# The last 96 columns of w1 streamed beside a block of wqkv, and their rows of w2 packed

## The chip, the cores and the metric

The kernel runs on one NeuronCore of a Trainium2 chip. The metric is the device time of one execution, in microseconds (us). Five engines work beside each other, each on its own list of instructions in a fixed order: TensorE (PE in the profile; its weight loads are PEld), VectorE (DVE), ScalarE (ACT), GpSimd (POOL) and SyncE (SP, which issues the DMAs here).

## The reference, cut to what matters

```
x = A_x                                  # [1, 2048, 512]
xn = layernorm(x)
# branch A: local dilated attention, 32 heads of 16, window 8, step 2
q, k, v = split(xn @ wqkv)               # wqkv [512, 1536]
logits = q . k[pos - 2*r], r = 0..7      # scaled, masked before position 0
s = (softmax(logits) . v[pos - 2*r]) @ wo
# branch B: MLP
y = layernorm(xn)
h = gelu(y @ w1 + b1)                    # w1 [512, 1376]
g = silu(h @ w2 + b2)                    # w2 [1376, 512]
return x + s * g
```

1376 is 10 blocks of 128 and one of 96. The last block is what the change is about.

## The kernel before, in words

**Layout.** The sequence is split by parity into two halves (c = 0, 1) of 1024 positions, since the window has step 2. A half is eight tiles i of 128 positions, with positions on the partitions for the attention. The normalised input y is also kept transposed, channels on the partitions, in `yT` (four pieces of 512 positions, one per MLP chunk `ch` = 0 to 3; half c holds chunks 2c and 2c + 1).

**Precision.** Every operand of a product is split in two fp16 parts, high and low, after a scaling with a power of two that is found at run time from its sum of squares (`sumsq`, `total`, `half_exp`, `up`, `down`; results in `qsc`, `hsc`, `zsc`, `osc`). A product is then three: high x high, high x low, low x high. ScalarE usually writes a high part, VectorE the low part (`split`), sometimes GpSimd.

**Attention.** There are eight units u = (c, hb): half c and a block hb of eight heads. `qkv(c, hb, u)` projects: for each tile, 12 products (3 x 4 blocks of 128 channels) with yT as the stationary operand and 384 columns of `wq` (q, k and v of these heads) streaming, into a PSUM bank of the ring `ps`; ScalarE (L763), in the first two units VectorE too (L759), writes the result into U[u % 2]. DMAs then copy the shifted edges. `attention` works on U on VectorE with elementwise products of 128 x 2048 (L805, L863) and reductions (L808), and GpSimd adds part of it (L873, L883). The products of unit u + 2 for a tile must wait until unit u has read that tile's v in the same U. The output goes in two parts through DMA transposes (L851) into `oT`.

**MLP.** For each chunk of 512 positions and each block f = 0 to 10 of 128 hidden channels, `mlp1` makes 12 products: a block of w1 stationary, 512 positions streaming, into a bank of `ps`; ScalarE applies bias and gelu (L1033) and writes the high part of h (L1036), VectorE the low part (L1038), into one of three buffers. `mlp2` makes, for each of the chunk's four tiles t, three products: h stationary, 512 columns of `w2` streaming, adding up in the four PSUM banks z0 to z3. The last block has 96 channels (M = 96 columns of the array) in `mlp1`; in `mlp2` its 96 rows and a row of ones against b2 make 97, in a tile of its own, `hlast`. After it silu empties the banks, and g goes to memory (`gd`).

```
nc.tensor.matmul(b.t[0:M], w1[:, s, f * 512 + k * M:f * 512 + (k + 1) * M], yT[ch][:, t, k],
...
nc.tensor.matmul(z.t, hl[s][0:K, t * P:(t + 1) * P], w2[0:K, w, f],
```

**Output.** `wo_first` multiplies half 0 with wo, in the middle; `wo_last` half 1 at the end: products over three of the four head blocks early, the last one late, after the last unit's transposes; then two VectorE passes (L993, L1000) and the output's DMA.

**Start.** `center`, `direct`: two tiles (6 and 7) come transposed from memory and are multiplied in fp32 without waiting for their normalisation; `ln0`, `second`, `y0`: statistics, normalisation and transposes of half 0; `prep_q`, `split`: weights. 24 filler products (WAKE, L1169) keep TensorE running.

**The order.** The program first collects all operations (`pl.add`) with what they read and write, and gives each a planned duration. `Plan.issue` then places them one by one, by a priority, on the engine where they can start first by those durations; that order is each engine's list. Constants at the head of the file (LOADS, HI_ENG, W1ENG, MLPN, PY and so on) choose engines and priorities. An engine's list is never changed at run time: an instruction that waits holds back all behind it.

Of the kernel before, what the change touches and what calls it, by code (L numbers as in the profile page):

```python
# [24 lines left out]
NI = 8  # L25
# [8 lines left out]
LASTPOOL = (0, 2, 4)  # L34

# [3 lines left out]
LAG = 2  # L39

# [4 lines left out]
BYDMA = (4, 5, 6, 7)  # L45
TRZ = (3, 3, 0, 2, 0, 1, 1, 0)
PTR = (0.5487, 0.3388, 0.0342, 0.6565, 0.7826, 0.1978, 0.0549, 0.9)
GROUPS = ((0,), (1, 2), (3, 4, 5), (6, 7))
BATCHES = ((0, 1, 2, 3, 4, 5), (6, 7))
LOADS = (('t', 6), ('q', 0), ('q', 2), ('x', 2), ('x', 0), ('q', 4), ('t', 7), ('x', 5), ('x', 1), ('x', 3), ('x', 4), ('q', 6), ('w', 0), ('w', 2), ('x', 7), ('c', 2), ('s', 1), ('c', 0), ('w', 3), ('x', 6), ('w', 1), ('c', 1), ('b', 0), ('s', 0))  # L50
HI_ENG = ('act', 'act', 'act', 'dve', 'dve', 'dve', 'dve', 'act')
XT = (0, 4, 30, 34)
Y_ENG = ('pool', 'act', 'dve', 'dve', 'act', 'pool', 'dve', 'act')

W1ENG = ('act', 'dve', 'act', 'act', 'act', 'act', 'act')
# [3 lines left out]
W2LO = ('dve', 'dve', 'dve', 'dve', 'dve', 'pool', 'dve')  # L59
EV0 = ('act', 'dve', 'dve', 'act', 'act', 'act', 'dve', 'dve')  # L60
EV1 = ('dve', 'dve', 'act', 'act', 'act', 'act', 'dve', 'act')
QLO0 = ('pool', 'dve', 'dve', 'pool')
QLO1 = ('dve', 'dve')
W1LO = ('dve', 'dve', 'pool', 'dve', 'dve', 'dve', 'dve')
WOLAG = 2
MEANBY = ('dve', 'pe', 'pool', 'pool')
W2LATE = 6

BEFORE_W1 = (0, 1, 4, 5)

# [26 lines left out]
class Plan:  # L97
# [89 lines left out]
    def place(self, o, t):  # L187

        if o.eng == "sp":
            if not o.nbytes:  # L190
                return t
            self.free["sp"] = t + o.issue
            self.dma = max(self.dma, t + o.issue + 0.3)
            self.dma += o.nbytes / (o.rate if self.dma > SLOW else 265e3)
            end = self.dma + o.tail
            self.landed.append((end, o.nbytes))
            return end
# [24 lines left out]
    def issue(self):  # L222
# [5 lines left out]
        order = []  # L228
        while len(order) < len(self.ops):
            best = None  # L230
            for e, cand in engs.items():
# [50 lines left out]
PW2 = 1.1284  # L282
PS2 = 0.4252
PWQ1 = 0.9
PW1 = 0.423
PB1 = 0.75
PCS = 0.6
PQ0 = 0.2677
PSQ0 = 0.1788
PMEAN = 0.04  # L290
PDIR = (0.192, 0.1517, 0.1187, 0.1556)
PG = (0.5671, 0.5205, 0.3952, 0.4033)
PY = (0.8339, 0.1477, 0.3649, 0.4824, 0.05, 0.5767, 0.05, 0.8333)
PU0 = 0.8687
PU1 = 0.969
PWARM = 0.9
PEV = 0.2698

PTOT = 0.5899

WAKE = 24
PS1 = 1.1561
# [3 lines left out]
PQLO = 0.5225  # L306

PFPLN = 0.35
PSEC = (0.6153, 0.7518, 0.1)

U1MH = 4
# [5 lines left out]
IORD0 = (6, 7, 0, 4, 1, 3, 2, 5)  # L317
IORD1 = (7, 0, 6, 3, 2, 4, 5, 1)
MLPN = (7, 7, 6, 4, 7, 7, 2, 0)
# [7 lines left out]
def tile_mixer(ctx, tc, a_x, a_xt, a_wqkv, a_wo, b_w1, b_b1, b_w2, out):  # L327
# [34 lines left out]
    ident = sb.tile([P, P], F32, name="ident")  # L362
    make_identity(nc, ident)
    fours = sb.tile([P, 2 * P], BF16, name="fours")
    nc.vector.memset(fours, 4.0)
    mean1 = sb.tile([P, P], F32, name="mean1")
    nc.vector.memset(mean1, 1.0 / D)
    halves = sb.tile([P, 16], F32, name="halves")
# [3 lines left out]
    misc = sb.tile([P, 512], F32, name="misc")  # L372
    v0 = misc[64:65]


    wq = sb.tile([P, NHB, 2, KT, 384], F16, name="wq")
    w1 = sb.tile([P, 2, KT * F], F16, name="w1")
# [6 lines left out]
    b1T = sb.tile([P, NF], F32, name="b1T")  # L384
    hlast = sb.tile([P, 2, 512], F16, name="hlast")
# [7 lines left out]
    R_mx = Ring(sb, [P, 64], F32, 4, "mx")  # L393
    R_cs = Ring(sb, [P, NI], F32, 8, "cs")
# [72 lines left out]
    def low_pool(n, lo, get, s, hi, **k):  # L467
# [4 lines left out]
        pool(0.45 + n * 3.9e-3, fn, **k)  # L472
# [36 lines left out]
    def scale_q(hb):  # L509
        col = R_s.new()  # L510
        for k in range(0, KT, 2):
            def go(k=k):
                src = stq[hb]()[:, k * 384:(k + 2) * 384]
                nc.scalar.activation(wq[:, hb, 0, k:k + 2].bitcast(BF16),
# [11 lines left out]
    def prep_q(hb):  # L526
# [3 lines left out]
        for k in range(0, KT, st):  # L530
            n = st * 384
            dst = [wq[:, hb, t, k:k + st].rearrange("p k e -> p (k e)") for t in range(2)]
            src = lambda k=k, n=n: stq[hb]()[:, k * 384:k * 384 + n]
# [117 lines left out]
    def y0(i):  # L651
# [12 lines left out]
        elif Y_ENG[i] == "pool":  # L664
            pool(1.25, lambda: nc.gpsimd.tensor_scalar(x(), x(), mv0[:, q, 0:1], rb0[:, q:q + 1], op0=ALU.subtract,
# [54 lines left out]

    def qkv(c, hb, u):
# [13 lines left out]
        raw = pl.users([("xc", j) for j in FP]) if u == 1 else set()  # L735
        csk = {i: (cs, g) for g in parts for i in g} if u == 0 else {i: cs for i in range(NI)}
        for n, i in enumerate((IORD0, IORD1)[u] if u < 2 else IORD):
# [5 lines left out]
            def mm(n0=0, n1=12, y=y, o=o, b=b):  # L743
                for n in range(n0, n1):
                    (s, t), k = ((0, 0), (1, 0), (0, 1))[n // KT], n % KT
                    nc.tensor.matmul(b.t[:, 0:384], y[:, s, k, o:o + P], wq[:, hb, t, k],  # L746
                                     start=(n == 0), stop=(n == 11))
# [4 lines left out]
            for n0, n1 in zip([0] + ends, ends):  # L752
                pe(n1 - n0, 384, lambda mm=mm, n0=n0, n1=n1: mm(n0, n1), [("yh" if n1 <= 4 else "y", c, i)] +
# [8 lines left out]
            else:  # L762
                act(384, lambda i=i, b=b: nc.scalar.activation(  # L763
                    U3[:, i:i + 31:15, :], b.t[:, 0:384].rearrange("p (t e) -> p t e", t=3),
                    AF.Identity, scale=cs.t[:, cp(i):cp(i) + 1]), **ev)

# [241 lines left out]
    def mlp1(ch, f):  # L1008
        M = P if f < NF - 1 else FL
# [15 lines left out]
        if f < NF - 1:  # L1025
            h = R_h.new()
            hi, lo = (lambda: h.t[:, 0]), (lambda: h.t[:, 1])
        else:
            h = ("hlast",)
            hi, lo = (lambda: hlast[:, 0]), (lambda: hlast[:, 1])  # L1030
        hk = (h, 0) if f < NF - 1 else ("hlast", 0)
# [9 lines left out]
        hq[f] = (hi, lo, M if f < NF - 1 else M + 1, h, hk)  # L1041

    def mlp2(ch, f):
        hi, lo, K, h, hk = hq.pop(f)
        for t in range(4):
# [3 lines left out]
            def mm(t=t, z=zt[t]):  # L1049
                hl = (hi(), lo())  # L1050
                for n, (s, w) in enumerate(((0, 0), (0, 1), (1, 0))):
                    nc.tensor.matmul(z.t, hl[s][0:K, t * P:(t + 1) * P], w2[0:K, w, f],  # L1052
# [314 lines left out]
```

## Time and profile before

| | |
|---|---|
| median of 3 runs | 415.07 us (414.49 to 415.13) |
| profiled execution | 415.18 us, its span 413.4 us |
| TensorE clock | 0.999 of full |
| DMA | 46.41 MB, mean 112 GB/s |
| GpSimd, ScalarE busy | 120.3 us, 222.1 us |

The span reaches from the first to the last instruction of the profiled execution. A group's row gives its line, engine, operation, output and inputs with shapes, the count, then the busy time in us and the mean ns of one, and then the engine's idle time just before these instructions with what ended most of it. Products overlap in the array, so the mean of one (from its start to its end) is longer than the distance from one to the next.

### The profile page before, as it was taken

How to read it: one execution, taken by the hardware profiler on the slowest of the kernel's cores; microseconds unless marked ns; L12 is line 12 of the kernel's file. 1: busy time of each engine (PE TensorE's matmuls, PEld its weight loads, DVE VectorE, ACT ScalarE, POOL GpSimd, SP SyncE). 2: the span in 40 equal slices, each digit the busy share in tenths (PEclk: the TensorE clock that was granted, in tenths of full speed). 3: DMA queues.
4: the chain of work that ended last, by engine and by line, in shares of the span. 5: the costliest groups of instructions: out<-in, count | busy, mean ns of one | idle time of the engine just before them, and what ended most of it. 6: DMA issues, size and time to landing. Idle time of an engine off the chain costs nothing.

```text
span 413.4 us, 5554 instructions
## 1 busy us (share of the span) xinstructions
PE 405.9 (98%) x2083; PEld 206.6 (50%) x2083; DVE 379.5 (92%) x379; ACT 222.1 (54%) x353; POOL 120.3 (29%) x131
## 2 busy tenths in 40 slices
PE   8799999999999999999999999999999999999996
PEld 5555544445654455445544554455455544444443
DVE  4996989998999999989998999999999998999954
ACT  4699899994549655843384252225212393263500
POOL 3834002004380425042504330434033404520021
PEclk9999999999999999999999999999999999999999
DMA  8958717030045137720172034223604244007133
GB/s 281 397 112 258 235 61 230 0 128 1 1 142 152 28 93 183 149 46 2 48 221 75 0 102 116 68 86 88 205 7 122 88 111 145 0 18 238 23 102 131
DMA packets 47211, 46.41 MB, mean 112 GB/s; under 512 B 31785, under 2 KB 32225, under 8 KB 46673
## 3 DMA queue, kind: packets, MB, share of 16 engines
q1 hardware_dynamic: 47184, 46.06, 37.6%
q8 instruction: 16, 0.26, 0.3%
q14 instruction: 11, 0.08, 0.1%
HBM read 24.06 MB, written 7.34 MB: 76 GB/s over the span
## 4 chain that ended last, share of the span: by engine, by line
PE 92%; ACT 3%; issue 1%; DVE 1%; POOL 1%; ACTq 0%
PE z L1052 28%; PE ps L1016 28%; PE ps L746 25%; PE ps L929 5%; PE ps L961 2%; PE z L961 2%; PE pl L746 1%; ACT w L421 1%; PE pl L961 1%; ACT f L673 1%; ACT yT L687 0%; ACT wq L536 0%; POOL wq L471 0%; POOL rb L635 0%; ACT prod L661 0%
## 5 line engine op out<-in xcount | busy, mean ns | idle before, releaser
L1016 PE MATMUL ps<-yT,w 128*128 128x512 f16 (+1 forms) x528 | 120.4, 379 | 0.0
L746 PE MATMUL ps<-wq,yT 128*128 128x384 f16 x708 | 117.0, 326 | 0.2 <-DVE U L759 0.2
L1052 PE MATMUL z<-w,h 128*128 128x512 f16 x480 | 110.4, 379 | 0.0
L746 PEld LDWEIGHTS <-yT 128*128 128x128 f16 x744 | 72.5, 98 | 49.2 <-issue 1.0
L1016 PEld LDWEIGHTS <-w 128*128 128x128 f16 (+1 forms) x528 | 52.8, 100 | 61.0
L805 DVE TENSOR_TENSOR prod<-U 128x2048 f32<-128x2048 f32 x32 | 73.2, 2286 | 2.2 <-POOL prod L883 0.7
L1052 PEld LDWEIGHTS <-h 128*128 128x128 f16 x480 | 46.6, 98 | 55.5 <-issue 0.3
L808 DVE TENSOR_REDUCE L<-prod 128x128 f32<-128x2048 f32 x32 | 73.0, 2281 | 0.4
L1033 ACT ACTIVATE ps<-ps,b1T,hsc 128x512 f32<-128x512 f32 (+1 forms) x44 | 32.9, 748 | 73.4 <-PE ps L1016 72.2
L863 DVE TENSOR_TENSOR prod<-pl,U 128x2048 f32<-128x2048 f32 x28 | 63.2, 2283 | 4.2 <-POOL prod L873 4.1
L763 ACT ACTIVATE U<-ps,cs 128x384 f32<-128x384 f32 x54 | 31.2, 580 | 65.2 <-PE ps L746 65.2
L873 POOL TENSOR_TENSOR prod<-prod,prod 128x2048 f32<-128x2048 f32 x7 | 31.7, 4531 | 113.8 <-DVE prod L863 99.6
L883 POOL TENSOR_TENSOR prod<-prod 128x1024 f32<-128x1024 f32 x14 | 32.9, 2349 | 0.0
L882 POOL COPY gate<-prod 1x1 f32<-1x1 f32 x21 | 5.5, 264 | 91.0 <-DVE prod L805 82.2
L1038 DVE SCALAR_TENSOR_TENSOR h<-ps,hsc,h 128x512 f16<-128x512 f32 x40 | 29.6, 741 | 1.7 <-ACT h L1036 1.4
L1036 ACT ACTIVATE h<-ps,hsc 128x512 f16<-128x512 f32 x40 | 27.3, 684 | 1.3 <-PE z L1052 0.4
L929 PE MATMUL ps<-wo,oT 128*128 128x512 f16 x96 | 21.7, 379 | 0.0
L858 DVE TENSOR_TENSOR prod<-prod,prod 128x2048 f32<-128x2048 f32 x9 | 20.5, 2282 | 0.0
L1033 ACT ACT_TABLE_LOAD x10 | 12.8, 1283 | 8.6 <-PE ps L1016 8.5
L883 POOL TENSOR_TENSOR prod<-prod,prod 128x1024 f32<-128x1024 f32 x7 | 16.4, 2347 | 0.0
L961 PEld LDWEIGHTS <-oT 128*128 128x128 f16 x108 | 10.6, 98 | 10.4
L929 PEld LDWEIGHTS <-oT 128*128 128x128 f16 x96 | 9.4, 98 | 11.2
(179 smaller groups left out, 377.8 us busy)
## 6 DMA issues: line engine op xcount, KB each, us to landing
f<-in_A_x_dram SPq DMA_DIRECT2D x31, 256.0 KB, 3.5
U<-U SPq DMA_DIRECT2D x16, 392.0 KB, 4.0
gd<-f SPq DMA_DIRECT2D x12, 256.0 KB, 3.4
prod<-in_A_x_dram SPq DMA_DIRECT2D x8, 256.0 KB, 6.9
oT<-in_B_w_dram SPq DMA_DIRECT2D x2, 1024.0 KB
yT<-in_B_w_dram SPq DMA_DIRECT2D x2, 1024.0 KB, 7.9
f<-gd SPq DMA_DIRECT2D x8, 256.0 KB, 2.7
out_dram<-f SPq DMA_DIRECT2D x8, 256.0 KB, 2.8
```

The source lines that it names most:

```text
L746: nc.tensor.matmul(b.t[:, 0:384], y[:, s, k, o:o + P], wq[:, hb, t, k], start=(n == 0), stop=(n == 11))
L763: act(384, lambda i=i, b=b: nc.scalar.activation(U3[:, i:i + 31:15, :], b.t[:, 0:384].rearrange("p (t e) -> p t e", t=3), AF.Identity, sca ...
L805: dve(2048, lambda p2=p2, g=g: nc.vector.tensor_tensor(p2(), q, slots(Ut, KH, 2 * g), op=ALU.mult), qk + [("kh", ub, 0), ("kh", ub, 1), (" ...
L808: dve(2048, lambda pr=pr, g=g: nc.vector.tensor_reduce(L3()[:, 2 * g:2 * g + 2], pr.t.rearrange("p (r f d) -> p r f d", r=2, d=DH), AX.X, ...
L863: dve(2048, lambda: nc.vector.tensor_tensor(pr.t.rearrange("p (r f d) -> p r f d", r=2, d=DH), A3()[:, 2 * g:2 * g + 2].rearrange("p r (f ...
L873: pool(4.75, lambda: nc.gpsimd.tensor_tensor(acc.t, acc.t, p1.t, op=ALU.add), [acc, p1], [acc])
L883: nc.gpsimd.tensor_tensor(x.t[:, 0:1024], x.t[:, 0:1024], y(), op=ALU.add)
L929: nc.tensor.matmul(b.t, oT[:, hb, i // 4, s, i % 4], wo[:, t, hb], start=(hb == 0 and n == 0), stop=(hb == last and n == 2))
L961: nc.tensor.matmul(b.t[:, cols], oT[:, hb, i // 4, s, i % 4], wo[:, t, hb, cols], start=(start and hb == 0 and n == 0), stop=(stop and hb ...
L1016: nc.tensor.matmul(b.t[0:M], w1[:, s, f * 512 + k * M:f * 512 + (k + 1) * M], yT[ch][:, t, k], start=(n == 0), stop=(n == 11))
L1033: act(512, lambda: nc.scalar.activation(b.t[0:M], b.t[0:M], AF.Gelu_apprx_tanh, bias=b1T[0:M, f:f + 1], scale=hsc[0:M, 1:2]), [b, ("b1T",) ...
L1052: nc.tensor.matmul(z.t, hl[s][0:K, t * P:(t + 1) * P], w2[0:K, w, f], start=(f == 0 and n == 0), stop=(f == NF - 1 and n == 2))
```

## The change

w1's last 96 columns move beside wqkv's third block (hb = 2, `HLAST`): `wq[2]` gets 480 columns, and the projection's products of the units u = 2 and u = 6 stream 480 columns in place of 384. So the last block of h is made with positions on the partitions, in the same PSUM bank as q, k and v (384 + 96 = 480 of 512). `mlp1` has no block 10 any more.

ScalarE takes the 96 columns out tile by tile into `hpt`. `last_block(ch)` then does for a chunk: GpSimd adds b1 (now also loaded as a row, spread over the partitions), ScalarE applies gelu and writes the high part twice, VectorE writes the low part in two pieces, and two DMA transposes bring it to channels on the partitions.

In `mlp2` the three products of 96 rows each (high x high, high x low, low x high: 288 rows, and b2) become two of 128 rows and one of 34: 96 rows of the high part with 32 of the low part, against w2's high part (96 rows of it and 32 of these again); the same 96 rows with the next 32 low rows, against w2's low part and 32 high rows; and the last 32 low rows with two rows for b2. The third product of one tile lies on rows 0 to 33, that of the next tile on rows 64 to 97, so tiles come in pairs (`pair`).

What goes with it: w2's last block is loaded and split in three forms (NX = 5 loads in place of 3, with one more sum of squares and four more passes); v's first row goes through DRAM (`v0`); `ident` and `mean1` share a tile with a buffer of the last block; rings `mx` and `cs` get smaller.

The order is now written out: `ORDER` lists all 1264 operations by the number under which the program adds them, and `Plan.issue` follows it. It can be read by counting the operations off in the source. TensorE's part around the third projection reads (M1 ch.f: first layer; M2 ch.f t: second layer, tile t; QKV u i: projection):

```
... | M1 1.0 | M2 0.7 t3 | QKV u2 i2 | M2 0.8 t1 | QKV u2 i7 | QKV u2 i4 | QKV u2 i3 | QKV u2 i1 | QKV u2 i6
| M2 0.9 t2 | QKV u2 i5 | QKV u2 i0 | M2 0.9 t1 | M1 1.1 | M2 0.8 t0 | M2 0.9 t0 | M2 0.8 t3 | M1 1.2
| M2 0.9 t3 | M1 1.3 | PAIR 0 23 | PAIR 0 01 | M1 1.4 | ...
```

ScalarE's behind the last of these tiles: `hp u2 i0 | sumsq of a tile | ev u2 i0 | attention 0 high half | gelu of block 10 | high part of block 10 | ...`. At the end TensorE has: `... | M2 3.9 | PAIR 3 23 | PAIR 3 01 | early 0 | early 3 | late 0 | late 3 | late 2 | early 5 | early 4 | late 5 | late 1 | early 6 | late 4 | late 6 | early 7 | late 7 | late 8`.

The constants are chosen anew too: five of seven high parts of w1 on VectorE (before: one), three low parts of w2 on GpSimd (before: one of another piece), the first tile's y on ScalarE (before: GpSimd), both means on TensorE, tile 2 in place of 4 transposed by DMA.

```diff
-BYDMA = (4, 5, 6, 7)
+BYDMA = (2, 5, 6, 7)
-Y_ENG = ('pool', 'act', 'dve', 'dve', 'act', 'pool', 'dve', 'act')
-W1ENG = ('act', 'dve', 'act', 'act', 'act', 'act', 'act')
+Y_ENG = ('act', 'dve', 'act', 'dve', 'act', 'act', 'dve', 'act')
+W1ENG = ('dve', 'dve', 'act', 'dve', 'dve', 'act', 'dve')
-W2LO = ('dve', 'dve', 'dve', 'dve', 'dve', 'pool', 'dve')
+W2LO = ('dve', 'dve', 'pool', 'pool', 'pool', 'dve', 'dve')
-QLO0 = ('pool', 'dve', 'dve', 'pool')
+QLO0 = ('pool', 'pool', 'pool', 'dve')
-W1LO = ('dve', 'dve', 'pool', 'dve', 'dve', 'dve', 'dve')
+W1LO = ('dve', 'dve', 'dve', 'dve', 'dve', 'dve', 'pool')
-MEANBY = ('dve', 'pe', 'pool', 'pool')
+MEANBY = ('pe', 'pe', 'pe', 'dve')
+ORDER = (
+    4, 18, 2, 0, 1, 3, 5, 36, 37, 38, 39, 111, 48, 122, 113, 117, 129, 131, 130, 120, 133, 132, 118, 126, 124,
...
+)
-        order = []
+        order, fixed = [], [self.ops[n] for n in reversed(ORDER)]
         while len(order) < len(self.ops):
             best = None
-            for e, cand in engs.items():
+            if fixed:
+                o = fixed.pop()
+                t = max([self.earliest(o)] + [min(b.ring.free) for b in o.bufs if b.slot is None])
+                assert not o.npred and t < float("inf")
+                best = (t, o)
+            for e, cand in engs.items() if best is None else ():
...
+    wq = [sb.tile([P, 2, KT, 384 + FL * (hb == HLAST)], F16, name=f"wq{hb}") for hb in range(NHB)]
+    w1 = sb.tile([P, 2, W1C[3]], F16, name="w1")
+    wl = wq[HLAST][:, :, :, 384:384 + FL]
...
+    def last_block(ch):
+        n = 4 * FL
+        h16 = R_f.new()
+        v = lambda: h16.t.bitcast(F16).rearrange("p (t a f) -> p t a f", a=2, t=4)
+        j = ch % 2
+        x = hpt[j][:, 0:n]
...
+            pool(1.0, lambda: nc.gpsimd.tensor_tensor(x3(), x3(), row, op=ALU.add), xk + [("b1T",)], xk)
+            act(n, lambda: nc.scalar.activation(x, x, AF.Gelu_apprx_tanh), xk, xk,
+                aps=1, table="gelu")
+            act(2 * n, lambda: nc.scalar.activation(
+                v()[:, :, :, 0:FL], x.rearrange("p (t o f) -> p t o f", t=4, o=1).to_broadcast([P, 4, 2, FL]),
+                AF.Identity, scale=hsc[:, 2:3]), xk + [("hsc2",)], [(h16, 0)])
...
+            low(lambda: v()[:, :, :, FL:P], 0, 2 * FR, (h16, 1))
+            low(lambda: hrem.rearrange("p a b (o f) -> p (a b) o f", o=2)[:, :, 0:1, 0:FR], 2 * FR, FL, ("hreml",))
+            dst = hlt[ch % 2].rearrange("p a (t x) -> p (a t) x", t=4)
+            dma(P * 2048, lambda: nc.sync.dma_start_transpose(dst, h16.t.bitcast(F16)), [(h16, k) for k in range(2)] + [("hreml",)],
+                [("hl", ch % 2)], rate=140e3, issue=1.3, tail=1.2)
+            dma(P * 512, lambda: nc.sync.dma_start_transpose(hlc[ch % 2], hrem.rearrange("p a b f -> p (a b f)")),
+                [("hreml",), ("hrem",)], [("hlc", ch % 2)], rate=140e3, issue=1.3, tail=1.2)
...
-                    nc.tensor.matmul(b.t[:, 0:384], y[:, s, k, o:o + P], wq[:, hb, t, k],
+                    nc.tensor.matmul(b.t[:, 0:wide], y[:, s, k, o:o + P], wq[hb][:, t, k],
                                      start=(n == 0), stop=(n == 11))
...
+        for a in range(0, 4, 2) if f == NF - 1 else ():
+            def pair(a=a, z=list(zt)):
+                ha = hlt[ch % 2].rearrange("p a (t x) -> p (a t) x", t=4)
+                for t in range(a, a + 2):
+                    for w in range(2):
+                        nc.tensor.matmul(z[t].t, ha[:, 2 * t + w], w2[:, w, f], start=False, stop=False)
+                for t in range(a, a + 2):
+                    r = slice(64 * (t - a), 64 * (t - a) + FR + 2)
+                    nc.tensor.matmul(z[t].t, hlc[ch % 2][r, a // 2], w2t[r], start=False, stop=True)
+            pe(5.3, 512, pair, [("hl", ch % 2), ("hlc", ch % 2), ("w2", f), ("w2t",)], [zt[a], zt[a + 1]])
...
-            if p < len(steps):
+            if p < len(steps) and steps[p][1] < NF - 1:
                 with prio(PR_M + p * 10):
                     mlp1(*steps[p])
```

223 lines of the change are left out of this document (137 added, 86 removed), and 61 rows, old and new, of the table ORDER.

## The prediction, on record before the change ran

> **What bounds the kernel now.** I read the page's busy shares and slices first, then the chain that ended last, then what TensorE waited for.
>
> ```profile
> PE 405.9 (98%) x2083; PEld 206.6 (50%) x2083; DVE 379.5 (92%) x379; ACT 222.1 (54%) x353; POOL 120.3 (29%) x131
> PE   8799999999999999999999999999999999999996
> DVE  4996989998999999989998999999999998999954
> PEclk9999999999999999999999999999999999999999
> 46.38 10.36 PE ps L1016 x48
> 101.60 15.60 PE ps L746 x96
> 119.14 2.59 PE ps L1016 x12
> 121.73 2.59 PE z L1052 x12
> 408.45 1.32 PE ps L961 x12
> PE z L683 <- POOL prod L665: 1.6, 1, 1.6
> PE z L683 <- DVE prod L668: 0.4, 1, 0.4
> ```
>
> The first row gives TensorE 98% and VectorE 92%: two engines are nearly full, in nearly every slice, and the clock is full throughout. The five rows of the chain (start, length, in us) show TensorE handing on to itself: 48 products of the first MLP layer in one piece at 46.38, 96 projection products from 101.60, the last 12 output products ending at 409.77. The two waits are TensorE's largest after its start, and both lie in the first 20 us. So the end is set by the sum of TensorE's products: a product removed anywhere after 20 us moves the end by its own length, as long as VectorE, with 8% to spare, keeps up. The rows of 12 give 2.59/12 = 215.8 ns for a product of 512 columns, the row of 96 gives 15.60/96 = 162.5 ns for 384 columns.
>
> **TensorE's sum.** Block 10 of the MLP (96 of 128 hidden channels) goes as a block.
>
> ```profile
> L1052 PE MATMUL z<-w,hlast 97*128 97x512 f16 x48 | 11.0, 379 | 0.0
> L1016 PE MATMUL ps<-yT,w 128*96 128x512 f16 x48 | 11.0, 379 | 0.0
> L599 PE MATMUL ps<-U,mean 128*128 128x128 f32 x8 | 1.2, 288 | 0.1
> L608 PE MATMUL ps<-f,mean 128*128 128x128 f32 x2 | 0.8, 501 | 0.1
> ```
>
> Removed: 48 products in each layer, full price although they use only 96 columns or 97 rows of the array: 96 x 215.8 ns = 20.72 us.
> Added in the projection: the eight tiles of wqkv's third block in each half of the sequence, 12 products each, 192 in all, now stream 480 columns. From 384 to 512 columns the price rises by 53.3 ns, so 96 columns cost 40.0 ns: 7.68 us.
> Added in the second layer: 16 tiles with two products of 128 rows, 32 x 215.8 ns = 6.91 us, and 16 products of 34 rows, issued in eight pairs, one of each pair on rows 0 to 33 and one on rows 64 to 97. No row shows products on separate rows. From below: the pair streams together, 8 x 215.8 ns = 1.73 us. From above: one after the other, and the array runs empty on entry and on leaving, 16 x (379 - 215.8) = 2.61 us more, 6.06 us in all (379 ns is one product from start to end). The 97-row row above says that fewer rows alone save nothing, and also that alternating 97 and 128 rows costs nothing: 11.0 us for 48 is the rate of the others. The halves use other rows and write other PSUM banks, so I take a tenth of the way up: 2.17 us.
> Sum: -20.72 + 7.68 + 6.91 + 2.17 = **-3.96 us**, between -4.40 and -0.07.
> The Trainium skill's "TensorEngine Tiling (Array Packing)", under "Tiling Modes", speaks against the pairs: a change of the tiling mode drains TensorE. By that rule the sum would lie near its end of -0.07 if every drain is exposed and the pair gains nothing else; the Trainium skill's "TensorE: Matmul & The Clock Gate", Part 3, has products on other rows start some 4 ns apart, which gives the end of -4.40. No run here shows either yet.
> The mean over channels of one early tile moves from VectorE (with one product) to four products on TensorE: 4 x 1.2/8 - 0.8/2 = +0.2 us.
>
> **The early part.** The first tile's normalisation moves from GpSimd to ScalarE.
>
> ```profile
> L665 POOL TENSOR_SCALAR prod<-prod,mv,rb 128x512 f32<-128x512 f32 x2 | 4.2, 2076 | 0.1
> L661 ACT ACTIVATE prod<-prod,rb 128x512 f32<-128x512 f32 x3 | 2.4, 813 | 0.1
> L1169 PE MATMUL z<-fours 128*128 128x256 bf16 x24 | 5.3, 389 | 1.2 <-DVE fours L365 1.2
> ```
>
> 2.08 us becomes 0.81 us ahead of the transpose for which TensorE waits 1.6 us. Against it, x's first tile and b1 are now loaded ahead of wqkv's first block. The whole order of the first 46 us is rewritten, and part of what it gains only replaces filler (24 products, 5.3 us). From both sides -1.6 to +1.5 us (the wait gone, or a wait as long for the later weights); I take -0.5.
>
> **VectorE, which must keep up.** The widened projection must wait for VectorE, because the first half's third block writes U0 and may start only when the first attention unit has read its last v from it.
>
> ```profile
> 43.99 2.28 DVE L805 TENSOR_TENSOR prod<-U 128x2048 f32<-128x2048 f32 x1
> 97.80 0.75 DVE L1038 SCALAR_TENSOR_TENSOR hlast<-ps,hsc,hlast 96x512 f16<-96x512 f32 x1 [1.89 <-ACT hlast L1036]
> 98.47 2.28 DVE L863 TENSOR_TENSOR prod<-pl,U 128x2048 f32<-128x2048 f32 x1
> L1038 DVE SCALAR_TENSOR_TENSOR h<-ps,hsc,h 128x512 f16<-128x512 f32 x40 | 29.6, 741 | 1.7 <-ACT h L1036 1.4
> L486 DVE SCALAR_TENSOR_TENSOR w<-yT,zsc,w 128x1024 f16<-128x1024 f32 x4 | 4.9, 1280 | 0.0
> L486 DVE SCALAR_TENSOR_TENSOR w<-f,zsc,w 128x512 f16<-128x512 f32 x1 | 0.7, 747 | 0.0
> L543 DVE SCALAR_TENSOR_TENSOR wq<-yT,qsc,wq 128x768 f16<-128x768 f32 x4 | 3.8, 986 | 0.0
> L480 DVE TENSOR_SCALAR w<-oT,hsc 128x512 f16<-128x512 f32 x1 | 0.5, 486 | 0.0
> L543 DVE SCALAR_TENSOR_TENSOR wq<-prod,qsc,wq 128x384 f16<-128x384 f32 x2 | 1.2, 610 | 0.1
> L602 DVE TENSOR_REDUCE f<-U 128x128 f32<-128x512 f32 x1 | 1.0, 1025 | 2.3 <-DMA U<-in_A_xt_dram 2.3
> ```
>
> Today that unit runs from 43.99 to 98.47 + 2.28 = 100.75, 56.8 us, and the projection starts 0.85 us later. By the written order TensorE reaches it sooner: ahead of it stand all of the first two projections, 11 blocks of the first MLP layer and 33 groups of three in the second, (132 + 99) x 215.8 ns = 49.9 us after 46.38, that is at 46.4 + 49.9 + 0.2 - 0.5 = 96.0. VectorE's list up to the same read has two low halves of h fewer (1.5 us), two w2 pieces in place of six (6.6 - 2.6 = 4.0) and none of the fourth projection block's (2.0): 7.5 us less. Ahead of its start it has more: w1's high halves for 3456 columns in place of 512, at 0.95 ns, +2.8; one low half of 1024 columns back and one of 384 gone, +0.7; the mean, -1.0, one low half of wqkv, -0.6: +1.9 us, if no idle time there takes it up. So the read ends between 44.0 + 49.3 = 93.3 and 95.2, before 96.0. Nothing is lost, with 0.8 us to spare.
> After that VectorE is about even: four low halves of 96 x 512 (3.0 us) go; eight pieces of 256 or 128 columns (some 0.47 and 0.33 us, on the line through 610 ns at 384 and 986 ns at 768) take their place, 3.2 us; w2's third form adds two passes over 512 columns, 0.49 + 0.75 us.
>
> **The new chain for the last block.** After the third block's last tile come an eviction of 96 columns, the bias on GpSimd, gelu, the high half, two low pieces and two DMA transposes, and only then the pairs, with everything after them on TensorE queued behind.
>
> ```profile
> L763 ACT ACTIVATE U<-ps,cs 128x384 f32<-128x384 f32 x54 | 31.2, 580 | 65.2 <-PE ps L746 65.2
> L703 ACT ACTIVATE f<-f,mv 128x512 f32<-128x512 f32 x8 | 5.7, 716 | 0.1
> L846 ACT ACTIVATE o<-prod,osc 128x1024 f16<-128x1024 f32 x7 | 8.0, 1141 | 2.7 <-POOL prod L883 2.7
> L536 ACT ACTIVATE wq<-yT,qsc 128x768 f16<-128x768 f32 x4 | 3.6, 921 | 0.0
> L421 ACT ACTIVATE w<-h 128x384 bf16<-128x384 f32 x1 | 0.5, 506 | 0.0
> L715 SPq DMA_TRANSPOSE yT<-f x8: 1232/1238/1630, 141.9 to 178.4; - x8
> DMA to landing us min/median/max: 3.0/3.1/3.7
> L851 SPq DMA_TRANSPOSE oT<-o x9: 1232/2003/2938, 127.0 to 393.8; - x9
> DMA to landing us min/median/max: 4.3/4.4/4.4
> ```
>
> Only the first occurrence is tight. ScalarE's list there: the 96 columns (0.3), a square over 512 (0.72, and 0.19 to read its sum), the other eviction (0.58), an attention output's high half (1.14), gelu over 384 (0.5), the high half over 768 (0.92). GpSimd's bias runs beside these; then VectorE 0.8 us; then two transposes, 1.24 us of issue each, the second landing 3.1 to 4.4 us after its own issue. Together 4.35 + 0.8 + 1.24 + 3.1 to 4.4 = 9.5 to 10.8 us. Cover on TensorE: three blocks of the first layer and five groups of three, 36 + 15 products, 11.0 us. It holds by 0.2 to 1.5 us. Without that cover a whole 10 us would show. The eight transposes also hold SyncE's queue for some 1.3 us each; behind them stand halo copies and reloads for later units, which have tens of us.
>
> **The tail.** The last unit's output must be transposed before the last quarter of the output product.
>
> ```profile
> 389.58 0.74 DVE L848 SCALAR_TENSOR_TENSOR o<-prod,osc,o 128x512 f16<-128x512 f32 x1
> 392.97 0.75 DVE L848 SCALAR_TENSOR_TENSOR o<-prod,osc,o 128x512 f16<-128x512 f32 x1 [0.79 <-ACT o L846]
> ```
>
> VectorE ends that unit's halves at 390.32 and 393.72; their transposes are there 4.4 us later, at 394.7 and 398.1. By the written order the second one's first user stands 7.2 us before TensorE's end (21 products of 512 columns and 24 of 256 at 1.32/12 us), at 398.6 if that end comes 3.96 us earlier: it fits by half a us. The first one's user stands 13.0 us before that end, at 392.8; VectorE's list brings that half forward by some 2.3 us, since the sums of the other half now follow it, so it lands at about 392.4. For this, the chain and the read of U0, each fitting closely, I add 0.4 us (0 to 2).
>
> **Total.** -3.96 + 0.2 - 0.5 + 0.4 = -3.86 us. The profiled execution took 415.18 us (span 413.4 and 1.8 around it), giving 411.3; the median of the runs is 0.11 lower, giving **411.2 us**.
>
> **Rivals.** *The pairs gain nothing.* If the small products run one after the other the sum is 16 x 0.2158 - 2.17 = 1.3 us poorer, and with the array empty at every change 3.9 us poorer: 412.5 to 415.1. For it: no row shows two products at once. Against it: other rows, other banks. 14%, half of it within the measurement. The drain rule of the Trainium skill's "TensorEngine Tiling (Array Packing)" ("Tiling Modes") speaks for this rival's later time.
> *VectorE is late with U0* (the slower side). If VectorE's list up to the last read of U0 gets none of the 7.5 us back, because it waits for ScalarE's halves in between (as it does for 1.89 us in the row of hlast) and starts 1.9 us later, the read ends at 102.7 and TensorE stands 6.7 us idle at 96.0, with a fixed list that lets it do nothing else: 411.2 + 6.7 = 417.9. It decides against the change from 4.7 us of lateness on, two products of 2.28 us. For it: 92% busy, strict lists, 0.8 us of room. Against it: the lists above, added up. 18%.
> *The early part gains its full room.* 9.2 us of the 409.8 before TensorE's last product hold no product that is needed (filler, waits, start). A third of it, 3 us, gone in place of 0.5: 408.7. For it: the wait on GpSimd is named. Against it: loads set the pace there. 14%.
>
> **How the numbers follow.** The forecast has 54%, its own range 410.0 to 412.9. The range for eight times in ten reaches from 408.3 (the early part) to 415.9 (drains exposed, with a close fit missed), leaving out most of VectorE's rival. A measurement of this kernel tells 0.2%, 0.8 us, from no change. Faster: 54 + 14 + 7 = 75%; within 0.2%: the other half of the first rival, 7%; slower: 18%.
>
> **What would show it.** Right: 192 products of 480 columns near 202 ns apart; TensorE without a wait near 96 and near 128 us; pairs whose two small products run side by side; TensorE's busy time near 402 us. Wrong: a TensorE wait for VectorE on the third projection block, a wait for the transposes ahead of the first pair, or a pair that takes over 0.6 us.

## The result and the profile after

| | before | changed |
|---|---|---|
| median | 415.04 us (4 runs) | 427.01 us (4 runs, 426.09 to 427.58) |
| ratio | | 1.029, interval [1.0275, 1.0303] |
| profiled execution, span | 415.18, 413.4 us | 426.09, 424.3 us |
| TensorE's last product ends | 409.8 us | 416.7 us |

2.9% slower, where 0.9% faster was forecast: 14.8 us between 411.3, the sum for the profiled execution, and 426.09. First the page of the changed kernel, with the busy times and the granted clock:

```profile
span 424.3 us, 5500 instructions
PE 405.0 (95%) x2041; PEld 199.6 (47%) x2041; DVE 391.9 (92%) x388; ACT 226.3 (53%) x374; POOL 128.1 (30%) x139
PEclk9999999999999999999999999999989999999998
```

TensorE is busy for 0.9 us less than before and its share falls from 98 to 95%: the time is lost around the products. VectorE has gained 12.4 us of busy time, of which the new instructions explain some 2 (381.4 in experiment 2, against 379.5 before). In the row of the clock, where each digit stands for one of 40 slices of the span, the slice from 308 to 318 us is below full; so is the last one, in most of which TensorE has ended. What TensorE waited for (in all, times, longest):

```profile
PE z L1184 <- DVE h L1159: 4.6, 2, 2.9
PE z L766 <- DVE prod L751: 1.5, 2, 0.9
PE ps L682 <- DMA U<-in_A_xt_dram: 1.4, 1, 1.4
PE ps L864 <- DVE h L1159: 1.0, 2, 0.7
```

Before, the longest wait was 1.6 us and all lay within the first 60 us. Now the low parts of h (L1159) come late. The groups of VectorE's instructions, shapes kept apart, say why (busy us, mean ns):

```profile
L930 DVE TENSOR_TENSOR prod<-U 128x2048 f32<-128x2048 f32 x32 | 77.2, 2415 | 2.3 <-ACT U L882 1.2
L827 DVE SCALAR_TENSOR_TENSOR f<-hl,hsc,f 128x256 f16<-128x256 f32 x2 | 5.2, 2619 | 0.0
L827 DVE SCALAR_TENSOR_TENSOR f<-first,hsc,f 128x256 f16<-128x256 f32 x2 | 1.0, 476 | 0.0
L569 DVE SCALAR_TENSOR_TENSOR w<-f,zsc,w 128x512 f16<-128x512 f32 x1 | 3.0, 2981 | 0.0
```

Two rows of one line, one shape and one engine differ by a factor of 5: 476 ns and a mean of 2619 ns. The timeline shows where the long one stands. VectorE, GpSimd and TensorE from 302 us on (start, length, idle time before in brackets):

```profile
302.48 4.76 DVE L827 SCALAR_TENSOR_TENSOR f<-hl,hsc,f 128x256 f16<-128x256 f32 x1
307.16 3.09 DVE L930 TENSOR_TENSOR prod<-U 128x2048 f32<-128x2048 f32 x1
310.17 0.74 DVE L1159 SCALAR_TENSOR_TENSOR h<-ps,hsc,h 128x512 f16<-128x512 f32 x1
```

```profile
302.44 4.51 POOL L998 TENSOR_TENSOR prod<-prod,prod 128x2048 f32<-128x2048 f32 x1 [11.10 <-DVE prod L988]
306.91 1.18 POOL L817 TENSOR_TENSOR first<-first,b1T 128x384 f32<-128x384 f32 x1
```

```profile
307.50 0.59 PE L1184 MATMUL z<-w,h 128*128 128x512 f16 x2
310.96 4.02 PE L1184 MATMUL z<-w,h 128*128 128x512 f16 x10 [2.87 <-DVE h L1159]
314.82 2.75 PE L1054 MATMUL ps<-wo,oT 128*128 128x512 f16 x12
```

VectorE's instruction, which reads two inputs from SBUF (on-chip memory), starts 0.04 us after GpSimd's sum and ends 0.29 us after it: 0.48 us of work became 4.76. The next one with two inputs in SBUF (L930, 2.28 us elsewhere) is held by the next GpSimd sum. The low part of h that TensorE needs stands behind both, TensorE idles for 2.87 us, and its next ten products take 3.86 us in place of 2.16, at half the clock. Here these two meetings together cost some 4.6 us. The Trainium skill's "Trainium Architecture — The Big Picture", under "What this means for kernel authors", calls the port pair that VectorE and GpSimd share an exclusive lock; the trace agrees, since the short instruction lasts until 0.29 us behind the sum. Beside the same sum in the kernel before stand an instruction with one of its inputs in PSUM and a reduction with a single input, at their usual lengths:

```profile
299.58 0.74 DVE L943 SCALAR_TENSOR_TENSOR f<-ps,osc,f 128x512 f32<-128x512 f32 x1
300.24 2.28 DVE L808 TENSOR_REDUCE L<-prod 128x128 f32<-128x2048 f32 x1
```

```profile
299.17 4.53 POOL L873 TENSOR_TENSOR prod<-prod,prod 128x2048 f32<-128x2048 f32 x1 [14.13 <-DVE prod L863]
```

The end of the changed kernel, GpSimd's last sum and then SyncE's nine outputs:

```profile
414.31 1.27 POOL L1122 TENSOR_TENSOR U<-U,f 128x512 f32<-128x512 f32 x1 [4.86 <-DVE U L1118]
```

```profile
415.61 5.74 SPq L1127 DMA_DIRECT2D out_dram<-U  x9
```

The written order puts the output of GpSimd's last sum first on SyncE, so all nine leave after 415.61; before, the first left at 399.6. From TensorE's last product to the end of the span there are 7.6 us in place of 3.6. Last, the pairs on TensorE:

```profile
130.16 1.03 PE L1172 MATMUL z<-w,hl 128*128 128x512 f16 x4
131.12 0.39 PE L1175 MATMUL z<-tail 34*128 34x512 f16 x2
131.44 1.04 PE L1172 MATMUL z<-w,hl 128*128 128x512 f16 x4
```

Four full products should take 4 x 0.216 = 0.86 us; the small ones start after 0.96. Both fit into 0.39 us, one product's length, so they run side by side, but the next full one starts 0.32 after them and not 0.22. The pair takes 1.28 us; six full products would take 1.29.

### The profile page after: what moved, and what is told of

Read it like the earlier page. It is cut to its first block, busy times and chain, and to the rows that moved or that the text cites. A ratio compares the mean times of both kernels' runs of the same rounds, so it can differ in the third digit from the quotient of the medians.

```text
span 424.3 us, 5500 instructions
## 1 busy us (share of the span) xinstructions
PE 405.0 (95%) x2041; PEld 199.6 (47%) x2041; DVE 391.9 (92%) x388; ACT 226.3 (53%) x374; POOL 128.1 (30%) x139
## 4 chain that ended last, share of the span: by engine, by line
PE 66%; DVE 15%; issue 7%; DMA 6%; ACT 2%; SPq 2%; POOL 1%; DVEq 0%; POOLq 0%
PE ps L864 23%; PE z L1184 16%; PE ps L1141 14%; PE ps L1054 5%; DVE prod L930 4%; DVE L L933 2%; DMA yT<-in_B_w_dram 2%; PE z L1086 2%; PE ps L1086 2%; PE z L1172 2%; DMA prod<-in_A_x_dram 2%; DVE prod L988 1%; DVE h L1159 1%; DVE w L569 1%; DMA yT<-f 1%
## 5 line engine op out<-in xcount | busy, mean ns | idle before, releaser
L864 PE MATMUL ps<-wq,yT 128*128 128x384 f16 (+1 forms) x720 | 130.4, 337 | 1.4 <-DVE h L1159 1.0
L1184 PE MATMUL z<-w,h 128*128 128x512 f16 x480 | 113.4, 383 | 4.6 <-DVE h L1159 4.6
L1141 PE MATMUL ps<-yT,w 128*128 128x512 f16 x480 | 109.7, 379 | 0.8 <-ACT U L882 0.5
L930 DVE TENSOR_TENSOR prod<-U 128x2048 f32<-128x2048 f32 x32 | 77.2, 2415 | 2.3 <-ACT U L882 1.2
L1141 PEld LDWEIGHTS <-w 128*128 128x128 f16 x480 | 46.7, 98 | 57.0 <-issue 2.4
L1154 ACT ACTIVATE ps<-ps,b1T,hsc 128x512 f32<-128x512 f32 x40 | 29.6, 746 | 38.3 <-PE ps L1141 38.0
L1159 DVE SCALAR_TENSOR_TENSOR h<-ps,hsc,h 128x512 f16<-128x512 f32 x40 | 29.4, 744 | 1.4 <-ACT h L1157 1.4
L971 ACT ACTIVATE o<-prod,osc 128x1024 f16<-128x1024 f32 (+1 forms) x9 | 9.5, 1051 | 18.8 <-POOL prod L1008 9.0
```

The source lines that it names most:

```text
L864: nc.tensor.matmul(b.t[:, 0:wide], y[:, s, k, o:o + P], wq[hb][:, t, k], start=(n == 0), stop=(n == 11))
L930: dve(2048, lambda p2=p2, g=g: nc.vector.tensor_tensor(p2(), q, slots(Ut, KH, 2 * g), op=ALU.mult), qk + [("kh", ub, 0), ("kh", ub, 1), (" ...
L1154: act(512, lambda: nc.scalar.activation(b.t[0:M], b.t[0:M], AF.Gelu_apprx_tanh, bias=b1T[0:M, f:f + 1], scale=hsc[0:M, 1:2]), [b, ("b1T",) ...
L1159: dve(512, lambda: nc.vector.scalar_tensor_tensor(lo()[0:M], b.t[0:M], hsc[0:M, 2:3], hi()[0:M], op0=ALU.mult, op1=ALU.subtract), [b, hk], ...
L1184: nc.tensor.matmul(z.t, hl[s][:, t * P:(t + 1) * P], w2[:, w, f], start=(f == 0 and n == 0), stop=False)
```

## The experiments

ORDER is written here by names: A3 pv0 is the first product of attention unit 3 with v, qk and red its products and reductions with k, lo a low part, LB the last block.

**1. The outputs' order.**

```diff
 SyncE, end of ORDER
-out4 out6 out5 out1 out3 out0 out8 out7 out2
+out2 out0 out3 out1 out5 out4 out7 out6 out8
```

> Only the order of SyncE's nine last output DMAs is changed: each stands in the order in which its sum is ready (tiles 2, 0, 3, 1, 5, 4, 7 first half, 6, 7 second half) in place of 4 first. Theory (the fixed list holds eight ready outputs behind tile 4's, whose sum GpSimd finishes at 415.6 us): the outputs are issued from about 408 us on, the time from TensorE's last product to the end of the span falls from 7.6 to about 3.7 us, and the kernel takes 427.0 - 3.9 = 423.1 us (422 to 424). Rival (the tail is long because nine outputs of 256 KB have to land): the tail stays within 1 us of 7.6 and the time above 426.

422.71 us (4 runs, 421.52 to 424.52), 4.3 less. SyncE now issues them from 410.19 on, beside TensorE's last products:

```profile
410.19 10.16 SPq L1127 DMA_DIRECT2D out_dram<-U  x9
```

So the tail's 4 us were the list on SyncE.

**2. VectorE beside GpSimd.**

```diff
 VectorE, three places in ORDER
-A1 qk1 ... (GpSimd's sum) ... A1 red1
+A1 qk1 | A1 red1
-A3 pv0 | hlo 2.2 | A3 pv1 | A4 qk0 | A4 red0 | hlo 2.1 | A3 pv3 | A3 pv2
+A3 pv0 | hlo 2.2 | A3 pv1 | A3 pv3 | hlo 2.1 | A4 qk0 | A4 red0 | A3 pv2
-A5 pv1 | A5 pv0 | LB2 lo32 | LB2 lo64 | A6 qk0 | hlo 2.8 | A6 red0 | A5 pv2
+A5 pv1 | LB2 lo32 | LB2 lo64 | A5 pv0 | hlo 2.8 | A5 pv2 | A6 qk0 | A6 red0
```

> Only VectorE's order is changed, in three places, so that no VectorE instruction with two operands in SBUF stands beside a GpSimd addition: the reduction of unit 1's second product goes ahead of w2's pieces; unit 3's third window product goes ahead of unit 4's first product; the last block's low pieces of chunk 2 go ahead of unit 5's second window product. Theory (VectorE is held by GpSimd's additions): the instructions of 2.98, 5.58, 4.76 and 3.09 us fall to 0.75, 2.3, 0.5 and 2.3 to 3.8 us, TensorE's waits of 0.7, 1.7 and 2.9 us for h go, with them the stretch at half clock (1.9 us), and the kernel takes 427.0 - 6.5 = 420.5 us (419 to 422.5). Rival (VectorE has more work by the last block's pieces and is late for that): the instructions get shorter but TensorE waits as long elsewhere, time above 425.

423.37 us (423.09 to 424.68), 3.6 less. The groups and TensorE's waits:

```profile
L827 DVE SCALAR_TENSOR_TENSOR f<-hl,hsc,f 128x256 f16<-128x256 f32 x2 | 1.0, 478 | 0.0
L569 DVE SCALAR_TENSOR_TENSOR w<-f,zsc,w 128x512 f16<-128x512 f32 x1 | 0.7, 732 | 0.0
```

```profile
PE ps L864 <- DVE f L1068: 1.7, 3, 0.7
PE ps L864 <- DVE h L1159: 1.1, 3, 0.5
```

The long instructions are back at their own length, but for one L930 of 3.07 us beside a GpSimd sum; VectorE's busy time is 381.4 us, the clock dip and the waits of 0.72, 1.72 and 2.87 us are gone. That GpSimd's sums hold these instructions is shown; the gain is 3.6 and not 6.5, since smaller waits for VectorE appear (2.8 us in these two rows).

**3. Both edits.**

> The two edits of the other runs together. Theory (two faults that follow each other in time): the gains add, 427.0 - 3.9 - 6.5 = 416.6 us (415 to 419), still not below the kernel before, because the start is 1.5 us later and the pairs of small products save nothing. Rival (one bound behind both): less than two thirds of the sum, above 420.

419.28 us (418.58 to 420.15), ratio 1.011 [1.0077, 1.0141]. The two gains add up (7.7 against 4.3 + 3.6), but 419.3 is above the forecast and still 4.4 us over the kernel before on that chip (414.87).

**4. Both small products on the same rows.**

```diff
-                    r = slice(64 * (t - a), 64 * (t - a) + FR + 2)
+                    r = slice(0, FR + 2)
```

> Both small products of a pair read rows 0 to 33 (the odd tiles get the wrong rows, so that part of the result is left out). Theory (on separate rows they start together, and each change between 128 and 34 rows costs 0.10 us): now the second starts 0.216 us after the first, and a pair takes 1.28 + 0.216 = 1.50 us. Rival (they run one after the other already, without any cost of changing): a pair stays at 1.28 us, the small ones 0.216 us apart.

```profile
131.61 0.60 PE L1175 MATMUL z<-tail 34*128 34x512 f16 x2
132.15 0.60 PE L1141 MATMUL ps<-yT,w 128*128 128x512 f16 x2
```

The next product starts 0.54 us after the small ones in place of 0.32, 1.50 us for the pair: side by side saves 0.22, and the 0.10 us at each change of rows stay. 426.68 us by one run.

**5. No change of rows.**

```diff
-                    r = slice(64 * (t - a), 64 * (t - a) + FR + 2)
+                    r = slice(0, FR + 66)
```

> Only the row ranges of the 34-row products differ: both products of a pair now use rows 0 to 97 of tile and weights, so TensorE works on all rows before, during and after them and never changes its division into row groups (the rows of two tiles are summed into one, so a part of the result is left out of what the reference wants). Theory (a change between all rows and a group of rows costs 0.10 us on the way in and on the way out, and this eats what packing saves): no 0.10 us gap, each small product lasts its 0.216 us, the pair of 4 full and 2 small products takes 6 x 0.216 = 1.30 us from its first start to the start of the next product, against 1.28 packed: within 0.03 us. Rival (the 0.10 us gaps belong to the switch of weights tile or of matrix, w2t and hlc, and not to the rows): gaps stay, the pair takes 1.50 us. As a whole like the changed kernel, 426 to 427.5 by one run.

```profile
130.86 1.03 PE L1172 MATMUL z<-w,hl 128*128 128x512 f16 x4
131.73 0.60 PE L1175 MATMUL z<-tail 98*128 98x512 f16 x2
132.16 1.03 PE L1172 MATMUL z<-w,hl 128*128 128x512 f16 x4
```

131.73 - 130.86 = 0.87 is four products exactly, and the pair takes 1.30 us. The gaps belong to the rows. A pair of two gains 0.216 by packing and pays 2 x 0.10: nothing is left. 426.82 us by one run.

**6. The planner's own order.** The changed kernel with `ORDER` empty and the constants of the kernel before.

> The changed kernel's blocks, tiles and products, but with the order of its operations not written out: the planner that the kernel before used chooses it, with that kernel's due times and choices of engine. Theory (what was lost is lost by the written order: VectorE instructions that read and write SBUF put beside GpSimd's sums, and SP's nine last transfers behind the slowest one): the planner keeps such pairs apart, so reductions stay at 2.2 to 2.3 us and L827 at 0.5 us, the outputs leave as they become ready, and the time falls by the 8 us that both written edits gave, to 415 to 420. Rival (the widening itself makes VectorE or the early part too late whatever the order): 424 or more, with waits of over 2 us of TensorE for VectorE. A third outcome, under 414, would say that the written order is worse than the planner's in places not yet found.

422.67 us (422.15 to 423.31): neither. GpSimd's sums stayed off L930, which has its usual length, but another wait came:

```profile
PE z L1184 <- ACT w L565: 4.3, 1, 4.3
PE z L1184 <- DVE w L569: 2.0, 1, 2.0
```

```profile
L930 DVE TENSOR_TENSOR prod<-U 128x2048 f32<-128x2048 f32 x32 | 73.0, 2287 | 1.1
PEclk9999997999999999999999999999999999999999
```

From 62.6 us on TensorE waits 6.3 us for the splitting of w2, and the seventh slice of the clock falls to 7 tenths. After 100 us it has no wait at all. So the widened blocks don't need the written order, and each order has its own place where it is late.

**7 and 8. VectorE lightened**, in the kernel before and in experiment 3's:

```diff
-nc.vector.tensor_tensor(p2(), q, slots(Ut, KH, 2 * g), op=ALU.mult)
+nc.vector.tensor_tensor(p2()[:, 0:1], q[:, 0:1], slots(Ut, KH, 2 * g)[:, 0:1], op=ALU.mult)
-L3()[:, 2 * g:2 * g + 2], pr.t.rearrange("p (r f d) -> p r f d", r=2, d=DH)
+L3()[:, 2 * g:2 * g + 2], pr.t[:, 0:1024].rearrange("p (r f d) -> p r f d", r=1, d=DH).to_broadcast([P, 2, 64, DH])
```

> The kernel before with half of VectorE's product of queries and keys left out: each instruction multiplies one of its two window rows, and the reduction reads that row twice, so half of the scores are wrong and 32 instructions of 2.28 us become about 1.15 us. VectorE loses 32 x 1.1 = 36 us of 379.5. It is the base for the next kernel. Theory (TensorE bounds the kernel before, waits for VectorE are 2 to 3 us in all and early): 414 to 415.5, unchanged within 0.3%. Rival (VectorE had a share in it): 411 or less.

414.99 us (10 runs), against 414.80 for the full one: ratio 0.9997 [0.9984, 1.0009]. VectorE had no share in the time before.

> The changed kernel with both corrections of its written order and with the same half of VectorE's products left out (half of the scores are wrong). VectorE loses about 36 us, so TensorE should not wait for it from 100 us on. Theory (the sum for TensorE holds but for the pairs: -3.96 + 1.3, and the early part is later by 1.5): TensorE ends at 409.8 - 3.96 + 1.3 + 1.5 = 408.6, the time is 413 to 415, 0 to 2 us below the lightened kernel before. Rival (TensorE's own work is longer than the sum, or the last 4 us over the kernel before in the corrected version are not VectorE's): 417 or more, near the corrected version's 419.3.

415.33 us (10 runs, 414.40 to 416.59), 4.0 less than experiment 3 (419.28, on another chip): that much of its time was VectorE's. A little over the expected 413 to 415, and level with the lightened kernel before, so TensorE's saving still didn't show. The largest waits that are left lie in the first 56 us:

```profile
PE ps L1141 <- ACT U L882: 1.9, 1, 1.9
PE z L1303 <- DVE first L440: 1.2, 1, 1.2
PE ps L682 <- DMA U<-in_A_xt_dram: 1.2, 1, 1.2
PE z L766 <- DVE prod L751: 1.1, 2, 0.6
```

With two small ones 5.9 us, 2.4 more than the 3.5 of the lightened kernel before. This profile is of the slowest of the ten executions (416.59), and in it TensorE's first products ran slower as well: eight of L682 take 2.08 us, in the changed kernel's profile 1.16.

```profile
5.51 2.08 PE L682 MATMUL ps<-U,first 128*128 128x128 f32 x8 [1.18 <-DMA U<-in_A_xt_dram]
```

```profile
5.62 1.16 PE L682 MATMUL ps<-U,first 128*128 128x128 f32 x8 [1.42 <-DMA U<-in_A_xt_dram]
```

So the new early part and the pairs' 1.2 use up the 4 us; how often the slow first products come was not measured.

**9 and 10. A new order, and the small products of a chunk together.** Both keep every operation and its engine. Number 9 has another `ORDER`, found with the planner's own durations, in which a GpSimd sum and a VectorE instruction with two inputs in SBUF exclude each other. Number 10 has one of the same kind and

```diff
 pair for a == 0: all eight full products of the chunk; for a == 2: all four small ones
-for t in range(a, a + 2):
+for t in range(4 if a == 0 else 0):
     for w in range(2): ...
-for t in range(a, a + 2):
-    r = slice(64 * (t - a), 64 * (t - a) + FR + 2)
+for t in range(4 if a == 2 else 0):
+    r = slice(64 * (t % 2), 64 * (t % 2) + FR + 2)
```

> The changed kernel, every operation, tile and choice of engine as it is, with only the written order (ORDER) replaced by one in which no VectorE instruction between two SBUF operands is put beside a GpSimd sum, the first loads, weights and their splits come in an order without TensorE waits of over 1.2 us, and the outputs leave as they become ready. Theory (all that was lost but the pairs' 1.3 us was lost by the order; nothing in the widened blocks themselves costs it): TensorE's waits fall from 11.7 us to 3 to 5, about the 3.4 of the kernel before, and its sum of -3.96 + 1.3 = -2.7 us shows: 414.9 - 2.7 + 0 to 1.5 = 412.2 to 413.7, ratio 0.993 to 0.997. Rival (VectorE, with 381 us of work, cannot keep up with a shorter TensorE list whatever the order, as the corrected version's 419.3 and its small waits may say): 415 or more, with waits for VectorE spread over the run after 100 us.

416.11 us (12 runs, 415.32 to 418.32), ratio 1.0031 [1.0018, 1.0044]. The theory's time is missed, and so is the rival's reason: behind 60 us no wait of TensorE is longer than 0.3 us. What is left is early (the profile is of the slowest of the twelve executions):

```profile
PE ps L864 <- ACT yT L770: 2.1, 1, 2.1
PE ps L864 <- ACT U L882: 1.0, 1, 1.0
```

```profile
PEclk9969999999999999999999999999999999999999
```

The 2.1 us end at 21.3 us, and the third slice of the clock is at 6 tenths.

> As the reordered kernel, with its own order of the same kind, and with the four 34-row products of a chunk behind all eight full ones in place of two behind each four: one change of rows each way for a chunk in place of two. Theory (0.10 us for each change of rows): four small products take 2 x 0.216 + 2 x 0.10 = 0.64 us from the end of the full ones to the next product, against 2 x 0.42 = 0.85 before, 8 changes less or 0.8 us in all: 411.4 to 412.9, TensorE's products some 0.8 us shorter. Rival (packed products gain only within one pair, or the cost stands at each small product): 0.85 us per chunk as before, and the time of the reordered kernel, or more since silu of two tiles starts later.

413.88 us (11 runs, 412.51 to 414.95), ratio 0.9967 [0.9953, 0.9981]: faster than both kernels, and above its expectation by the early part again (a wait of 1.5 us near 20 us, the third slice of the clock at 8 tenths). The four small products:

```profile
132.66 0.61 PE L1175 MATMUL z<-tail 34*128 34x512 f16 x4
133.20 2.76 PE L1141 MATMUL ps<-yT,w 128*128 128x512 f16 x12
```

With 0.10 on the way in, 0.54 + 0.10 = 0.64 us, where two pairs pay 0.85: the cost stands at the change of rows, once each way. Of the 2.2 us between 9 and 10 this explains 0.8; the orders differ too.

**11 and 12. Filler where TensorE waits.** Number 10 with eight of its filler products moved from between the first projections to the waits at 17 to 21 us, three in place of each.

```diff
-wake | ... | wake x2 | ... | wake x3 | ... | wake | ... | tr1 | wake | tr3 | QKV u0 i3 | tr4
+wake x3 | tr1 | wake x6 | tr3 | wake x12 | QKV u0 i3 | wake x3 | tr4
```

> The grouped kernel with eight of its 24 filler products moved and made three each: they no longer stand between products that could run (10 to 17 us), but where TensorE waited, ahead of the second to fifth transpose and the projection behind them (17 to 21 us). Nothing else differs. In the grouped kernel TensorE is granted half its clock from 21.2 to 24.6 us, right behind waits of 0.5, 0.4 and 1.5 us, and its products of that time take twice as long: 3.4 / 2 = 1.7 us. Theory (the idle time ahead of it brings the half clock): it goes, the waits themselves stay as idle or filler time, 413.9 - 1.7 = 411.7 to 412.7. Rival (the clock dips whatever TensorE does there, or fillers hold back the products that follow as much as they save): 413.5 or more.

The profiled execution took 412.31 us, without the dip, as the theory has it; but in four of the eleven executions of number 10 the mean granted clock is 1.000 too (0.996 with the dip in its profile), so that one profile doesn't settle it. The other five took 416.0 to 416.8 (median of all six 416.12). A second profile was to show why:

> The same kernel as the last one, for a second profile: its profiled execution took 412.31 us, its other five 416.0 to 416.8, and the difference of 3.7 to 4.5 us is not explained by the trace of the short one. Theory (the clock: without fillers between 10 and 17 us TensorE gets its full clock later, or loses it again there): a longer execution shows 6.8 to 8.9 us more at half clock before 30 us, and nothing else changed. Rival (a load: x's first tiles land later, which the fillers have nothing to do with): a TensorE or VectorE wait for a DMA of 2 to 4 us in the first 20 us, at full clock.

416.55 us (on another chip), and neither: its first 30 us are the same to within 0.02 us, clock included. The two profiles part at 294 us. VectorE and GpSimd, in the short execution, then in the long one:

```profile
294.29 2.29 DVE L930 TENSOR_TENSOR prod<-U 128x2048 f32<-128x2048 f32 x1
```

```profile
294.44 6.54 POOL L998 TENSOR_TENSOR prod<-prod,prod 128x2048 f32<-128x2048 f32 x1 [0.63 <-DVE prod L988]
```

```profile
294.89 6.12 DVE L930 TENSOR_TENSOR prod<-U 128x2048 f32<-128x2048 f32 x1 [0.69 <-DMA U<-U]
```

```profile
294.35 4.51 POOL L998 TENSOR_TENSOR prod<-prod,prod 128x2048 f32<-128x2048 f32 x1 [0.62 <-DVE prod L988]
```

In these two, whoever starts first holds the other off. In the first, VectorE is 0.15 us ahead and GpSimd's sum is stretched by 2 us, which nobody waits for. In the second a DMA lands 0.6 us later, GpSimd is ahead, VectorE is held, and TensorE waits 2.75 us at 304 and loses the clock again: 4.2 us from half a microsecond. The other five executions of that length were not profiled. In three of them the mean granted clock is 1.000, against 0.996 in this profile, so they lost their time in another way, without half a clock. Whether the moved filler has to do with the later DMA is open.

Nor do the recorded starts always decide. In the changed kernel's profile a VectorE instruction starts 0.10 us ahead of a GpSimd sum, and VectorE is the one that is held (2.98 us in place of 0.73); GpSimd's copy just before the sum was still running then. Whether that is the reason is not shown.

```profile
97.91 0.79 POOL L1007 COPY gate<-prod 1x1 f32<-1x1 f32 x1 [6.49 <-DVE prod L930]
98.56 2.98 DVE L569 SCALAR_TENSOR_TENSOR w<-f,zsc,w 128x512 f16<-128x512 f32 x1
98.66 2.34 POOL L1008 TENSOR_TENSOR prod<-prod 128x1024 f32<-128x1024 f32 x1
```

## Why the prediction was wrong, step by step

- **The step that failed: "as long as VectorE, with 8% to spare, keeps up", "VectorE is about even".** The instructions were counted rightly: with the three places mended VectorE has 381.4 us against 379.5. That their length depends on what GpSimd does at that moment was not asked, although the written order is fixed and GpSimd's sums stood in it. After 100 us TensorE waited 6.0 us, 5.6 of it for VectorE (0.4 in all was allowed for close fits), and lost 1.7 us to the clock: +7.3 us. Experiment 2 shows 3.6 us of it to come from the held instructions; experiment 8, with a shorter list for VectorE, another 4.0 us. That this rest lies in the written order and not in the amount of VectorE's work is shown by experiments 6 and 9: with 380.6 and 381.7 us of it TensorE waits after 100 us for VectorE by 0.2 us at most. One of the prediction's own signs of being wrong is in the changed kernel's trace: on the third projection block, at 106.35 us, TensorE waits 0.72 us for VectorE, for a low part of h that stands behind the instruction held at 98.56.
- **The tail.** The two transposes were looked at and fit; SyncE's list behind them was not read. +4.0 us, shown by experiment 1.
- **The early part.** Taken at -0.5. TensorE's idle time up to 60 us rose from 3.8 to 5.7 us, by 1.9 and outside the bound of +1.5: +2.4 us. Experiments 8 to 10 show that waits there are what is left when the rest is mended; which load or engine choice makes them is open.
- **The pairs.** "A tenth of the way up" gave 0.27 us for two small products; they take 0.42: 3.4 in place of 2.17 us, +1.2, within the bounds given (1.73 to 6.06). With the 1.7 us at half clock this is why TensorE's busy time is 405.0 and not the 402 that were to be seen. The Trainium skill's two rules hold at once: products on other rows start some 4 ns apart ("TensorE: Matmul & The Clock Gate", Part 3), here 3 to 4 ns, and a change of the mode drains the array ("TensorEngine Tiling (Array Packing)", "Tiling Modes"), here for 0.10 us. The argument from the 97-row products failed: they pay nothing for the change since they don't use a group of rows (experiment 5).
- Together 7.3 + 4.0 + 2.4 + 1.2 = 14.9, against 14.8 measured.

What held: the products of 480 columns (2.43 us for twelve, 202.5 ns each); U0, whose last v is read by 91.8 us, before TensorE asks at 97.5; the chain for the last block, whose first pair starts at 130.16 without a wait; and the sum for TensorE but for the pairs, which number 10 shows in part.

Of the rivals, *VectorE is late with U0* had the right side and engine, and the wrong place: U0 was on time, the low parts of h were not. *The pairs gain nothing* was true, and small. None of the three had GpSimd's sums, which hold VectorE off, or SyncE's list.

## What to carry to other kernels

Before a written order is trusted, lay GpSimd's list beside VectorE's: a VectorE instruction with two inputs in SBUF that meets a GpSimd sum can cost up to that sum's whole length, and a few tenths of a microsecond decide which of the two is held. Read each queue to its last entry: in a list served in order, one that isn't ready holds back all behind it. Row packing paid here from the second pair between two changes of rows on, since a change cost half of what a packed pair of 512 columns saved.

## What the runs showed of the hardware

- 0.48 us of VectorE work became 4.76 us beside a GpSimd sum of 4.51 us; a GpSimd sum of 4.51 us became 6.54 us behind a VectorE product of 2.29 us that was 0.15 us ahead.
- A change between all rows and 34 rows costs 0.10 us each way, whether the two small products lie on the same rows or on separate ones (experiments 4 and 10); between 128 and 98 rows it costs nothing (experiment 5).
- A TensorE wait of 2.87 us cost another 1.7 us through half a clock (ten products in 3.86 us in place of 2.16), one of 2.75 us in experiment 12 another 1.4 (ten in 3.61). With filler products in waits of 0.4 to 1.5 us near 20 us the clock was full there in both profiles taken; number 10, without them there, fell to 8 tenths in that slice of its profile, but four of its eleven executions have a mean clock of 1.000.
